# Seven quadrant products instead of eight in the second MLP product of a sparse-attention and mixer kernel

## The chip, the cores and the metric

The kernel runs on one core of a Trainium2 chip. The time is the device time of one execution in microseconds. Medians are over several executions; traces come from the hardware profiler. In a trace, PE is TensorE's matmul, PEld its weight load, DVE is VectorE, ACT ScalarE, POOL GpSimd and SP SyncE. Clock shares beside the spans are between 0.98 and 1.00 of full speed in all profiles used here but one, which is marked.

## The reference, cut to what matters

```python
# batch 4, heads 8, seq 768, head_dim 64; x = attention output, (4, 768, 512)
keep = is_global | is_local                 # 8 global keys, 96 local ones
a = softmax(where(keep, q @ k.T / 8 + bias, -1e9));  x = a @ v
h = x.transpose(0, 2, 1) @ U @ V            # U (768, 32), V (32, 768): mixer of rank 32
u = x + h.transpose(0, 2, 1)
ch = np.maximum(u @ w_ch1, 0.0) @ w_ch2     # w_ch1 (512, 2048), w_ch2 (2048, 512)
return u + ch
```

Batches are worked on one after the other. Attention of batch b+1 lies beside the MLP of batch b. Heads go in pairs, so there are 16 pairs, numbered over all batches. An evacuation is a copy of a result out of PSUM, the memory that TensorE writes to; the kernel uses PSUM as eight banks of 512 fp32 columns.

## The kernel before

Every piece of work is a `Task` with an engine, a duration, a priority and dependencies. A planner, run when the program is built, turns the tasks into one fixed instruction order per engine. Tasks that need a buffer or a PSUM bank acquire a `Group`. The framework then sets the semaphores for that order from what each instruction reads and writes. The second MLP product is one accumulation of 16 row blocks of 128 for each of six token tiles, each in a bank of its own. The residual u comes as x on VectorE and as the mixer's rank-32 part in a row-tiled matmul (one on 32 or 64 rows; several run side by side. One on 128 rows is called full-height).

```python
banks = [Group("ps", among=MLP1) for _ in units]      # a PSUM bank for each token tile
...
o = ps[:, g.slot, 0:c1 - c0]
for jc in range(lo, hi_):                             # 16 matmuls of 512 columns
    nc.tensor.matmul(o, htr[:, jc, tt * P:(tt + 1) * P], w2[:, jc, c0:c1],
                     start=False, stop=(jc == NJC - 1))
...
def rest(ahead=tuple(ahead)):                         # mixer part of the residual, 32 rows
    nc.tensor.matmul(ps[:, banks[u].slot, 0:a1 - a0], vrep[r, t2 * P:(t2 + 1) * P],
                     tb[r, a0:a1], start=True, stop=False)
...
def fin(...):                                         # one sum for each tile
    nc.vector.tensor_tensor(osb[go.slot][:, c0:c1], ps[:, g.slot, 0:c1 - c0], xb[:, tt, c0:c1], ALU.add)
```

The softmax here doesn't subtract the row's maximum and nothing guards it: scores larger than these inputs give would overflow.

## Time and profile before

| | before |
|---|---|
| median time | 242.29 us (242.01 to 242.84) |
| first matmul of the first MLP product | 33.19 us |
| start of the last matmul | 237.39 us, and 3.19 us from there to the end |
| TensorE's gaps between those two | none over 0.25 us |

A gap here, and everywhere below, is what the distance between the starts of two matmuls in a row has beyond the usual pace. It is a little more than the idle time that the views of the profile print, as matmuls overlap. What the prediction shows of this kernel is not shown again. Two more places matter later. The first is the page's throughput of DMA in 40 slices of the span (6 us each):

```profile
GB/s 172 161 181 210 114 142 199 210 174 129 159 181 196 185 161 181 117 96 38 109 155 123 142 156 157 3 0 3 2 85 48 44 87 3 0 0 4 122 53 87
```

The fifth slice, 24 to 30 us, has 114 GB/s: transfers run through the start. The second is the tail, from the timeline (start, duration, engine, line, operation, and in brackets the idle time before it):

```profile
237.34 0.96 SPq L871 DMA_DIRECT2D out_dram<-osb  x2
237.65 0.29 DVE L866 TENSOR_TENSOR osb<-ps,x_sb 128x128 f32<-128x128 f32 x1 [0.34 <-PE ps L834]
```

The last sum is of 128 columns only and its store is 64 KB.

### The profile page before, as it was taken

What the parts mean: (1) busy time and instruction counts of PE and PEld (TensorE: products, weight loads), DVE (VectorE), ACT (ScalarE), POOL (GpSimd) and SP (SyncE); (2) the same over time, 40 slices, a digit from 0 to 9 for tenths busy, and PEclk for the clock granted to TensorE, in tenths of its full rate; (3) what the DMA queues carried; (4) which work ended last, traced back from release to release, by engine and by line L of the source; (5) the groups of instructions that cost most, each with busy time, mean ns of one, the idle gap of its engine ahead of it and who ended that gap; (6) DMA issues with size and microseconds to landing.
All of it is one profiled execution on the core that took longest, in us unless ns stands there. A gap on an engine that the chain in (4) does not pass through costs nothing.

```text
span 240.6 us, 4943 instructions
## 1 busy us (share of the span) xinstructions
PE 232.8 (97%) x2092; PEld 129.8 (54%) x2092; DVE 96.7 (40%) x181; ACT 109.2 (45%) x141; POOL 91.3 (38%) x118
## 2 busy tenths in 40 slices
PE   7889799999999999999999999999999999999995
PEld 3546666566445655665545546655456456654443
DVE  5968852233364642330557852433336410001221
ACT  3786859875224028657243338567220026660000
POOL 8996994549961960190081910300001000000000
PEclk9999999999999999999999999999999999999999
DMA  8999899999999999895499996000021120000312
GB/s 172 161 181 210 114 142 199 210 174 129 159 181 196 185 161 181 117 96 38 109 155 123 142 156 157 3 0 3 2 85 48 44 87 3 0 0 4 122 53 87
DMA packets 89910, 26.39 MB, mean 110 GB/s; under 512 B 77760, under 2 KB 86912, under 8 KB 89888
## 3 DMA queue, kind: packets, MB, share of 16 engines
q0 software_dynamic: 65696, 13.24, 68.3%
q1 hardware_dynamic: 24192, 12.83, 26.2%
q8 instruction: 16, 0.26, 0.5%
q14 instruction: 6, 0.05, 0.1%
HBM read 27.46 MB, written 6.29 MB: 140 GB/s over the span
## 4 chain that ended last, share of the span: by engine, by line
PE 88%; DMA 5%; POOL 3%; DVE 2%; issue 0%; SPq 0%; POOLq 0%; DVEq 0%
PE ps L834 36%; PE ps L794 35%; PE ps L602 4%; DMA stgq<-in_q_dram 4%; PE ps L675 2%; PE ps L653 2%; PE ps L658 2%; PE ps L674 2%; PE ps L847 2%; DMA stg<-in_q_dram 2%; PE ps L754 2%; POOL x L739 1%; PE ps L895 1%; PE ps L499 1%; POOL vt L389 1%; DVE bias L340 1%
## 5 line engine op out<-in xcount | busy, mean ns | idle before, releaser
L834 PE MATMUL ps<-w,htr 128*128 128x512 f16 (+2 forms) x400 | 88.6, 371 | 0.0
L794 PE MATMUL ps<-uT,w 128*128 128x384 f16 x512 | 87.8, 326 | 0.0
L811 ACT ACTIVATE htr<-ps 128x768 f16<-128x768 f32 x64 | 51.9, 811 | 37.0 <-PE ps L794 37.0
L794 PEld LDWEIGHTS <-w 128*128 128x128 f16 x512 | 48.3, 98 | 32.0 <-issue 0.5
L613 ACT ACTIVATE ep<-ps 128x1024 f16<-128x1024 f32 (+1 forms) x48 | 44.4, 952 | 39.4 <-PE ps L602 38.0
L834 PEld LDWEIGHTS <-htr 128*128 128x128 f16 x400 | 36.1, 98 | 41.5 <-issue 3.8
L866 DVE TENSOR_TENSOR osb<-ps,x_sb 128x512 f32<-128x512 f32 (+2 forms) x25 | 16.7, 670 | 54.4 <-PE ps L834 54.2
L739 POOL CAST x<-x_sb 128x768 f16<-128x768 f32 x12 | 10.6, 888 | 53.2 <-DVE x_sb L713 25.4
L626 DVE TENSOR_TENSOR ep<-ep,mask 128x1024 f16<-128x1024 f16 x24 | 17.4, 725 | 30.6 <-ACT ep L613 30.6
L389 POOL DMA_DIRECT2D vt<-in_v_dram x16 | 16.5, 1033 | 23.7 <-PE ps L675 22.3
L296 POOL COPY vo<-vt 32x650 f16<-32x650 f16 x22 | 17.1, 782 | 6.6 <-DMA vt<-in_v_dram 6.0
L385 POOL DMA_DIRECT2D stgk<-in_k_dram x20 | 16.6, 838 | 4.1 <-DMA w<-in_moe_w_ch_dram 1.7
L385 POOL DMA_DIRECT2D stgq<-in_q_dram x20 | 16.5, 835 | 3.2 <-DMA w<-in_moe_w_ch_dram 1.7
L602 PEld LDWEIGHTS <-kT 64*128 64x128 f16 x352 | 9.9, 94 | 11.9 <-issue 10.4
L294 DVE CAST uT<-ps 128x768 f16<-128x768 f32 (+1 forms) x15 | 12.3, 845 | 8.6 <-PE ps L754 8.6
L602 PE MATMUL ps<-qT,kT 64*128 64x128 f16 x352 | 15.7, 218 | 0.0
L713 DVE TENSOR_TENSOR x_sb<-ps,rcp 128x768 f32<-128x768 f32 x16 | 15.3, 956 | 0.6
L292 ACT ACTIVATE uT<-ps 128x384 f16<-128x384 f32 (+1 forms) x5 | 2.8, 555 | 24.8 <-PE ps L754 24.8
L675 PEld LDWEIGHTS <-ep 128*128 128x128 f16 x192 | 12.4, 97 | 1.9
L675 PE MATMUL ps<-vt,ep 128*128 128x65 f16 x192 | 13.2, 193 | 0.0
L622 DVE TENSOR_TENSOR ep<-ep,mask 128x768 f16<-128x768 f16 x12 | 6.9, 573 | 14.9 <-ACT ep L613 14.9
L674 PE MATMUL ps<-vo,ep 128*128 128x65 f16 x160 | 11.9, 193 | 0.0
(57 smaller groups left out, 146.3 us busy)
## 6 DMA issues: line engine op xcount, KB each, us to landing
out_dram<-osb SPq DMA_DIRECT2D x23, 256.0 KB, 2.0
w<-in_moe_w_ch_dram POOLq DMA_DIRECT2D x8, 512.0 KB, 11.8
vt<-in_v_dram POOLq DMA_DIRECT2D x16, 192.0 KB, 8.1
stgk<-in_k_dram POOLq DMA_DIRECT2D x20, 96.0 KB, 8.7
stgq<-in_q_dram POOLq DMA_DIRECT2D x20, 96.0 KB, 7.1
vo<-vt SPq DMA_DIRECT2D x13, 121.9 KB, 6.8
stgk<-in_k_dram POOLq DMA_DIRECT2D x5, 192.0 KB, 5.1
stgq<-in_q_dram POOLq DMA_DIRECT2D x5, 192.0 KB, 5.9
```

The costliest lines, as they stand in the source:

```text
L296: nc.gpsimd.tensor_copy(dst, src)
L385: nc.gpsimd.dma_start(o[:, :, hi], src[b, h0 + hi].rearrange("(n p) d -> p n d", p=P))
L389: nc.gpsimd.dma_start(vt[gv.slot][:, :, :, 0:D], v[b, h0:h0 + 2].rearrange("h (n p) d -> p h n d", p=P),)
L602: nc.tensor.matmul(t[:, hi, j * P:(j + 1) * P], lhs, qt[r, i * P:(i + 1) * P], start=not biased, stop=True, skip_group_check=biased,)
L613: nc.scalar.activation(ep[gep.slot][:, :, lo:512], ps[:, gsc.slot:gsc.slot + 2, lo:512], AF.Exp, scale=qk_scale)
L626: nc.vector.tensor_tensor(ev, ev, mv, ALU.mult)
L674: nc.tensor.matmul(o, e[:, hi, j * P:(j + 1) * P], vof[:, hi, i - 1], start=True, stop=False)
L675: nc.tensor.matmul(o, e[:, hi, (j + 1) * P:(j + 2) * P], vv[:, hi, i], start=(i == 0), stop=True)
L794: nc.tensor.matmul(ps[:, g.slot + half, 0:HS], w1[:, dc, jt * P:(jt + 1) * P], ub[:, dc, half * HS:(half + 1) * HS], start=(dc == 0), stop ...
L811: nc.scalar.activation(htr[:, jt].rearrange("p (h c) -> p h c", h=2), ps[:, g.slot:g.slot + 2, 0:HS], AF.Relu)
L834: nc.tensor.matmul(o, htr[:, jc, tt * P:(tt + 1) * P], w2[:, jc, c0:c1], start=False, stop=(jc == NJC - 1),)
L866: nc.vector.tensor_tensor(osb[go.slot][:, c0:c1], ps[:, g.slot, 0:c1 - c0], xb[:, tt, c0:c1], ALU.add)
```

## The change

The intent is to save an eighth of the multiplications of the second product. Its three matrices are cut in halves both ways, and the 2x2 product of blocks is done with seven block products and some sums (the scheme of Strassen and Winograd). The sums of the relu's output (`sA`, and in place in `htr`), of the weights (`tB`, and in place in `w2`) and of the products are on VectorE. ScalarE takes the mixer's evacuations in the later batches, scores come in two groups a pair instead of three, the mixer's small products become full-height, and the durations of the sums in the plan are measured ones.

For each of three pairs of token tiles there are now four accumulators of 256 columns. **They lie two to a bank:** `gX` holds P1+P2 and P6, `gY` holds P7 (later P4) and P5 (later P3).

```diff
-        banks = [Group("ps", among=MLP1) for _ in units]
+        for t in range(ht):
+            gX, gY = Group("ps", 3, among=among), Group("ps", 4, among=among)
+            def half(g, i):
+                return ps[:, g.slot, i * hd:(i + 1) * hd]
 ...
+            P1 = prod(1, gX, 0, htr[:, 0:hj], w2[:, 0:hj, 0:hd], ..., 1)
+            P6 = prod(6, gX, 1, sA[:, 1], tB[:, 0], pa[0::2] + c_tb, 2)
+            P7 = prod(7, gY, 0, htr[:, 0:hj], tB[:, 1], pa[1::2] + c_ta, 3, c0=HS)
+            P5 = prod(5, gY, 1, sA[:, 0], w2[:, 0:hj, hd:DM], pa[0::2] + c_ta, 4)
+            D0 = ...  # ScalarE: u2 = P1          D1 = ...  # u2 += P6
+            D2 = ...  # u3 = P7 + u2              D4 = ...  # x22 += P5
+            P2 = prod(2, gX, 0, htr[:, hj:NJC], w2[:, hj:NJC, 0:hd], ... + [D0], 5)
+            P4 = prod(4, gY, 0, htr[:, hj:NJC], tB[:, 2], ... + [D2], 6, c0=HS)
+            P3 = prod(3, gY, 1, sA[:, 2], w2[:, hj:NJC, hd:DM], ... + [D4], 7)
+            D3 = ...  # x22 += u3                 D5 = ...  # x12, x21 += u2 (512 columns)
+            D6, D7, D8 = ...  # x11 += P1+P2, x21 += P7+P4, x12 += P5+P3
 ...
+        p1 = add(DVE, 1.16, ..., pre1, ...)   # two fp16 sums of quadrants of htr
+        p2 = add(DVE, 1.06, ..., pre2, [p1])  # two more; four times a batch
 ...
-            e = {"A": ACT, "D": DVE}[CFG.get("E", "DDD")[p]] if first else DVE
+            e = {"A": ACT, "D": DVE}[CFG.get("E", "DDD")[p] if first else CFG.get("EB", "A")]
 ...
-CFG = {'petr': (4, 5), 'cast0': 'AD', 'E': 'DAD', 'VO': 'DPPSSSSSSSSSSSSS'}
+CFG = {'petr': (4, 5, 6), 'E': 'DAD', 'VO': 'PPSSSSSSSSSSSSSS'}
```

The priorities of the plan are all new as well, so the order of nearly everything moves a little.

## The prediction

> **What bounds the kernel now.** I read the page's busy table first, then its slices, then the chain that ended last.
>
> ```profile
> PE 232.8 (97%) x2092; PEld 129.8 (54%) x2092; DVE 96.7 (40%) x181; ACT 109.2 (45%) x141; POOL 91.3 (38%) x118
> ...
> PE   7889799999999999999999999999999999999995
> ...
> PEclk9999999999999999999999999999999999999999
> ...
> PE 88%; DMA 5%; POOL 3%; DVE 2%; issue 0%; SPq 0%; POOLq 0%; DVEq 0%
> ```
>
> TensorE is at 9 tenths from the sixth slice to the last but one, at full clock, and 88% of the chain is its own work. A busy PE need not be a PE at its peak, so I looked at what it does. The groups of instructions:
>
> ```profile
> L834 PE MATMUL ps<-w,htr 128*128 128x512 f16 (+2 forms) x400 | 88.6, 371 | 0.0
> L794 PE MATMUL ps<-uT,w 128*128 128x384 f16 x512 | 87.8, 326 | 0.0
> ...
> L866 DVE TENSOR_TENSOR osb<-ps,x_sb 128x512 f32<-128x512 f32 (+2 forms) x25 | 16.7, 670 | 54.4 <-PE ps L834 54.2
> ```
>
> L834 is the second MLP product, L794 the first. Together they are 71% of the chain, with no idle time before them. The 371 ns is a latency and overlaps its neighbours, so rates must be read from start times. The waits of TensorE sum to under 5 us in the whole run, all before 33.2 us, when the first matmul of L794 starts. From there to the last matmul at 237.6 us the kernel is TensorE's queue, so a microsecond taken from TensorE there is one taken from the time, as long as the other engines keep up. The table of stretches, with the columns PE, PEld, DVE, ACT, POOL, shows their slack (first product and second product of batch 0, then of batch 1, then the second product of batch 3):
>
> ```profile
> 33.19:59.36 26.17, 26.17 (x258) 16.05 (x254) 7.58 (x14) 20.16 (x28) 16.65 (x21) 1.00 1.61 175
> 59.36:87.90 28.54, 28.54 (x235) 14.22 (x234) 14.83 (x26) 6.62 (x8) 20.31 (x25) 1.00 1.90 170
> 87.90:111.90 24.00, 24.00 (x197) 14.30 (x194) 6.00 (x11) 15.50 (x19) 8.15 (x10) 1.00 1.34 131
> 111.90:142.10 30.20, 30.20 (x291) 15.53 (x291) 18.39 (x32) 10.46 (x12) 13.61 (x16) 1.00 1.18 127
> ...
> 215.10:240.60 25.50, 22.51 (x120) 10.41 (x119) 4.31 (x7) 0.81 (x1) 0.00 (x0) 1.00 0.17 63
> ```
>
> VectorE is used for 22 of the 55 us of batch 0's MLP and 24 of the 54 us of batch 1's.
>
> The timeline of the last batch gives rates and the price of a small group:
>
> ```profile
> 230.12 3.63 PE L834 MATMUL ps<-w,htr 128*128 128x512 f16 x16
> ...
> 233.68 0.09 PEld L847 LDWEIGHTS <-vrep 32*128 32x128 f16 x2 [0.42 <-issue]
> ...
> 233.94 3.50 PEld L834 LDWEIGHTS <-htr 128*128 128x128 f16 x32 [0.17 <-issue]
> ```
>
> From 230.12 to 233.68 there are 16 matmuls and one entry into 32-row matmuls: 3.56 us. Another stretch has 56 matmuls from 217.61 to the next entry at 229.81, 12.20 us. The difference, 40 matmuls in 8.64 us, is 0.216 us for one, which leaves 0.10 us for the entry. At 217.29 two 512-column matmuls run side by side in separate row groups and the full-height ones resume at 217.61: 0.32 us less 0.216 is 0.10 us for the exit. So **each run of row-tiled matmuls costs about 0.20 us beside its columns**.
>
> **What the Trainium skill says.** "TensorE: Matmul & The Clock Gate", section "Back-to-back issue gap", has 134, 262 and 518 cycles for 128, 256 and 512 columns, 56, 109 and 216 ns at 2.4 GHz. The trace agrees where it can: 0.216 us at 512, and six 128-column matmuls with six weight loads in 0.34 us (L653); it has no 256-column one. "TensorEngine Tiling (Array Packing)", section "Key Properties", says that a change of tiling mode drains TensorE; the 0.10 us each way is that. "VectorE: DVE Perf Modes", section "The TRN2 errata — SBUF-src ops pay a fixed extra latency per instruction", gives an fp32 sum of two tensors as (N+151)/0.96 ns: 692 ns for 512, measured 691 (L866). At 256 it gives 424 ns. "SBUF — State Buffer" says that a VectorE operation with two SBUF inputs is blocked by a GpSimd operation that reads SBUF. The mask product usually takes 0.69 us, but 1.16 at 69.56 us, beside a GpSimd copy: agrees.
>
> **The change part by part.** All on TensorE after 33 us.
>
> 1. Second product, per batch: 6 token tiles x 16 matmuls x 0.216 = 20.7 us becomes 7 products x 3 tiles x 8 = 168 matmuls of 256 columns, at 0.109 (estimate, between 0.0555 for 128 and 0.1625 for 384 columns of L794) = 18.3 us. Four batches: 83.0 - 73.2, **-9.8 us**. The eighth saved would be 10.4; the rest is the fixed cost of twice-as-many, smaller matmuls.
> 2. Residual products (L847): 13 groups of parallel 32-row matmuls at 0.216 = 2.8 us become 12 groups of four full-height 256-column ones at 0.436 = 5.2: **+2.4**.
> 3. Mixer product (L754): 12 after 33 us, from two 384-column matmuls side by side (0.163) to two in sequence (0.326): **+2.0**.
> 4. Pair 6 gets its transposes on TensorE in place of DMA: 24 of about 0.033 (such a set takes 0.79 at 32.4 us): **+0.8**.
> 5. Row-tiled runs: after 33.2 us I count 39 on TensorE's timeline: 25 with scores, 14 of residual or mixer products alone. The latter become full-height and stop being runs. Scores of batches 1 to 3 come in two groups a pair instead of three: 24 at most, some adjacent, say 22. 17 x 0.20: **-3.4**.
>
> Sum: -9.8 + 2.4 + 2.0 + 0.8 - 3.4 = **-8.0 us**. Note that 2 and 3 are paid for by 5, so nearly all of the eighth survives.
>
> VectorE pays. Per batch: 16 sums of two fp16 quadrants of 768 elements (0.55 us, like the 0.57 of the 768-element mask product) = 8.9; per tile seven 256-element fp32 sums at 0.42 and one of 512 at 0.65 = 3.6, for three tiles 10.8; off go six 0.69 sums (4.2) and three mixer evacuations of 0.95 in batches 1 to 3 (2.9), which ScalarE takes at 0.81. Batch 1: 24.4 + 8.9 + 10.8 - 7.1 + 0.3 = 37 of now about 52 us. Batch 0 adds the sums of the second weights (8 of 0.7: 5.6): 41 of about 53, 78%. In all VectorE goes from 97 to about 155 us, ScalarE from 109 to about 121. Neither becomes the bound on average.
>
> At the ends: the tail has a 0.42 us sum in place of 0.29 and a store of 128 KB in place of 64: **+0.3**. In the first 33 us, where VectorE is busy for 25, the four 0.82 us vrep casts (3.3) give way to four half-length pieces (about 1.9) and an early memset: **-0.3**, uncertain in sign.
>
> **The rivals.**
>
> A: *VectorE becomes the bound locally.* For: batch 0's second product needs both weight-sum sets, which wait for the last of the w loads, and has the densest attention work beside it; about 27 us of VectorE work falls in 26 us there if little is moved ahead; GpSimd copies and casts collide with the new two-SBUF-input sums, as at 69.56 us. VectorE is a strict queue: one sum waiting for a product holds the masks behind it. Against: only 7.6 us of VectorE in the 26 us before, PSUM groups allow the first products of two tiles (plain operands) to run first, and the order was planned with these durations. I charge **+1.0 us** in the centre; if it went badly, 4 to 6 us, a time of 238 to 240.
>
> B: *256-column matmuls don't reach 0.109*, because each now needs its own 98 ns weight load. Were the pace 0.12, 672 x 0.011 = 7.4 us of gain is gone: about 241. Against: L653 sustains one load and one matmul in 0.056 us. Unlikely.
>
> C: *The start decides*: any lateness of the first L794 comes through in full. The plan's priorities are all different, so +-1 us.
>
> D: *First products of a batch wait for the last relu and its sums.* About 0.3 + 0.81 + 1.16 and hand-overs, some 2.7 us, against residual, first and second plain products of two tiles, 4.3 us, on TensorE. Hidden, even in batch 3 where no attention fills in.
>
> **The number.** 242.3 - 8.0 + 0.3 - 0.3 + 1.0 = 235.3, which I round to 235.2 (2.9% faster). Spread: +-0.8 us for the runs of row mode, +-1 for the start, -1 to +4 for VectorE waits: 232.6 to 238.6 should hold it 8 times in 10. Faster by over 2% means under 237.4; only rival A or B at size prevents that: 0.80. Within 2%: 0.18. Slower: 0.02.
>
> **What would show it.** 672 matmuls of 256 columns with starts 0.108 to 0.11 us apart (step 1); no 32-row matmuls and 20 to 24 row-tiled runs after the start (2, 3, 5); VectorE at 145 to 165 us busy; TensorE still without gaps from 33 us on, waits on VectorE under 2 us in total (A), the first L794 within 1 us of 33.2 (C). I am wrong if TensorE waits on VectorE for more than 3 us, if the fp16 sums take well over 0.6 us, or if the first product starts much later.

## The result, and the profile after

The median is 240.49 us (239.86 to 240.64) against 242.15 us of the kernel before in the same rounds. The ratio is 0.9923, with a 95% interval of 0.9893 to 0.9952. Ratios here are the mean time of one kernel's fast runs over that of the other's fast runs of the same rounds, so not quite the ratio of the medians quoted. The change is 0.8% faster, within 2%, and the time lies above the predicted range.

The page of the kernel after, busy times first, then the DMA throughput and the engines of the chain that ended last:

```profile
PE 226.9 (95%) x2436; PEld 165.8 (69%) x2436; DVE 146.8 (62%) x317; ACT 122.9 (52%) x165; POOL 90.6 (38%) x116
...
GB/s 169 167 131 137 39 166 200 201 209 187 164 154 168 206 184 191 175 103 61 119 58 164 128 164 195 0 3 0 3 1 91 88 90 2 0 3 0 0 91 176
...
PE 70%; DMA 17%; DVE 8%; issue 1%; POOL 1%; SPq 0%; DVEq 0%; ACT 0%; POOLq 0%
```

TensorE's share of the chain fell from 88% to 70%, while DMA rose from 5 to 17 and VectorE from 2 to 8. TensorE's own part of the time did shrink, and waits took most of it back. What TensorE waited for in the whole run (total, times, longest), the largest lines:

```profile
PE ps L734 <- DMA vo<-vt: 2.2, 1, 2.2
PE ps L934 <- DVE x_sb L947: 1.5, 2, 1.0
...
PE ps L934 <- DVE w L508: 0.9, 1, 0.9
...
PE ps L855 <- DVE x_sb L947: 0.3, 1, 0.3
PE ps L934 <- DVE u L947: 0.3, 1, 0.3
```

L934 is the second product, L855 the first, L947 the sums of products, L508 a sum of weights. The first line lies before the MLP starts. The others are waits of TensorE on VectorE, 3.0 us, inside the part that had none before. Counted from start to start there are six gaps, 4.16 us: 1.04 at 65.1 us (the weight sum), and 0.46, 0.54, 0.29, 1.15 and 0.68 at 123.3, 141.2, 188.0, 190.3 and 227.5 us (sums of products; for the one at 188.0 us this view names no releaser).

From the start times, with the measured sizes beside the predicted ones:

| step | predicted, us | measured, us |
|---|---|---|
| second product, without waits (mean pace of each size times its count: 83.2 and 73.4) | -9.8 | -9.8 |
| all else of TensorE after the start (residual, mixer, pair 6, runs of row-tiled matmuls) | +1.8 | +1.5 |
| waits on VectorE | +1.0 | +4.16 |
| first matmul of the first MLP product | -0.3 | +1.07 (34.26 against 33.19) |
| from the last matmul's start to the end | +0.3 | +1.06 (4.25 against 3.19) |
| sum | -7.0 | -2.0 (the spans are 238.6 and 240.6) |

The table of stretches, for the second product of batches 0 and 1 (columns as in the prediction):

```profile
59.10:89.10 30.00, 29.13 (x373) 24.31 (x371) 28.45 (x60) 11.67 (x16) 25.65 (x31) 1.00 2.02 177
112.60:141.80 29.20, 28.59 (x366) 24.33 (x365) 22.82 (x51) 11.85 (x17) 13.28 (x15) 1.00 1.20 120
```

VectorE is busy for 28.45 of 30.00 us in the second product of batch 0 (and for 10.49 of the 24.84 us before it, so 71% of the two; the prediction counted 78%). Yet none of the five gaps on sums of products is in batch 0. They lie in batches 1 to 3, where VectorE has room. The timeline of the last one, in batch 3 where no attention is left, shows why:

```profile
225.02 1.04 PE L934 MATMUL ps<-w,sA 128*128 128x256 f16 x8
...
225.90 1.04 PE L934 MATMUL ps<-w,htr 128*128 128x256 f16 x8
226.10 0.42 DVE L947 TENSOR_TENSOR u<-ps,u 128x256 f32<-128x256 f32 x1 [0.38 <-PE ps L934]
...
226.77 1.04 PE L934 MATMUL ps<-tB,htr 128*128 128x256 f16 x8
...
227.84 0.76 DVE L947 TENSOR_TENSOR x_sb<-ps,x_sb 128x256 f32<-128x256 f32 x2 [0.72 <-PE ps L934]
228.32 0.93 PE L934 MATMUL ps<-w,sA 128*128 128x256 f16 x7 [0.52 <-DVE x_sb L947]
```

The product at 225.02 is P5, in the second half of `gY`. It ends at 226.06, and the sum at 226.10 starts just then; but this sum (D2) reads P7 in the first half, which had ended at 224.3, and VectorE had been idle for 0.38 us. P4 follows at 226.77, into the first half. The sum that reads P5 (D4) could have run once VectorE was free, but it starts at 227.84, just after P4's end at 227.81, with VectorE idle for 0.72 us. P3, which must follow D4, so starts late. A sum of one half waits for the product that writes the other half, and the next product into the bank waits for the sum. The wait at 190.3 us is of the same kind: P4 of that tile, which needs only D2 (ended at 190.71), starts at 191.56, just after the sum of the other half ended at 191.51:

```profile
187.27 0.69 DVE L970 TENSOR_TENSOR x_sb<-x_sb,u 128x512 f32<-128x512 f32 x1
187.88 0.42 DVE L947 TENSOR_TENSOR x_sb<-ps,x_sb 128x256 f32<-128x256 f32 x1
...
188.35 1.03 PE L934 MATMUL ps<-tB,htr 128*128 128x256 f16 x8
...
190.29 0.42 DVE L947 TENSOR_TENSOR u<-ps,u 128x256 f32<-128x256 f32 x1 [1.74 <-PE ps L934]
...
191.09 0.42 DVE L947 TENSOR_TENSOR x_sb<-ps,x_sb 128x256 f32<-128x256 f32 x1
...
191.56 1.03 PE L934 MATMUL ps<-tB,htr 128*128 128x256 f16 x8 [0.98 <-DVE x_sb L947]
```

The five gaps are not all alike. Before those at 141.2, 190.3 and 227.5 us VectorE stood idle for 1.17, 1.74 and 0.72 us, though the product that its next sum reads had ended 0.9 us or more before that sum began. The one at 141.2 us is indirect: the late sum (D7) holds up the sum behind it in VectorE's queue, and that one frees the bank for the next batch. Before the gaps at 123.3 and 188.0 us VectorE had no pause of over 0.1 us in the 1.6 us before the wait ended. There the shared bank is why TensorE must wait for that sum at all (P3 for D2, and P7, at 188.35, for D4), and the work ahead of the sum in VectorE's queue is why it comes late.

"PSUM — Partial Sum Buffer" of the Trainium skill has the likely reason in its section "PSUM bank collisions raise a hardware error": two engines must not be in one bank and quadrant at the same time, even in disjoint columns, and the rule is "Semaphore-guard PSUM by **bank × quadrant** (by bank is the simple version), not by address". The waits in the trace are what one would expect of guards set by bank. This is the theory called BANK in the records below. Its rival LOAD says that VectorE is too full, and that sums come late because others stand before them.

The tail, from the same timeline of the kernel after:

```profile
232.47 3.43 SPq L978 DMA_DIRECT2D out_dram<-x_sb  x5
...
233.56 1.04 PE L934 MATMUL ps<-w,sA 128*128 128x256 f16 x8
234.63 0.76 DVE L947 TENSOR_TENSOR x_sb<-ps,x_sb 128x256 f32<-128x256 f32 x2 [1.32 <-PE ps L934]
```

Two sums, not one, wait for the last matmul; one of them reads the other half of the bank, whose product had ended 0.9 us earlier. Five stores are issued in the last microseconds, and a sum of 256 columns with 256 KB behind it takes the place of one of 128 with 64 KB.

The start, from the chain in order of time (start, duration, what):

```profile
16.76 4.11 DMA vo<-vt
...
26.74 0.97 DVE x_sb L773
27.75 0.09 issue
27.84 0.82 POOL x L799
28.65 0.70 POOL w L443
29.35 7.88 DMA w<-in_moe_w_ch_dram
```

The first weights are issued by GpSimd at 28.6 us, behind a cast that hangs on attention's results. The last line shown is the second of these loads; from there the chain runs over later loads to the weight sum before the gap at 65 us. The page has 39 GB/s in the fifth slice, against 114 before. The kernel before issues its first weights at 12.2 us, and they land at 21.35; here they land at 34.03. The theory START says that the order of the loads costs the microsecond.

### The profile page after: what moved, and what is told of

It reads as the page before. It is cut to its first block, busy times and chain, and to the rows that moved or that the text cites. A ratio compares the mean times of both kernels' runs of the same rounds, so it can differ in the third digit from the quotient of the medians.

```text
span 238.6 us, 5808 instructions
## 1 busy us (share of the span) xinstructions
PE 226.9 (95%) x2436; PEld 165.8 (69%) x2436; DVE 146.8 (62%) x317; ACT 122.9 (52%) x165; POOL 90.6 (38%) x116
## 4 chain that ended last, share of the span: by engine, by line
PE 70%; DMA 17%; DVE 8%; issue 1%; POOL 1%; SPq 0%; DVEq 0%; ACT 0%; POOLq 0%
PE ps L934 29%; PE ps L855 27%; DMA w<-in_moe_w_ch_dram 11%; PE ps L646 3%; DMA vt<-in_v_dram 3%; PE ps L735 2%; PE ps L922 2%; DMA vo<-vt 2%; PE ps L734 2%; DMA sA<-in_q_dram 2%; PE ps L813 2%; PE ps L718 2%; PE ps L713 2%; DVE x_sb L947 1%; DVE x_sb L773 1%
## 5 line engine op out<-in xcount | busy, mean ns | idle before, releaser
L855 PE MATMUL ps<-uT,w 128*128 128x384 f16 x512 | 86.4, 326 | 0.3 <-DVE x_sb L947 0.3
L855 PEld LDWEIGHTS <-w 128*128 128x128 f16 x512 | 48.8, 98 | 32.3 <-issue 0.3
L934 PEld LDWEIGHTS <-htr 128*128 128x128 f16 x384 | 36.7, 98 | 6.9 <-issue 1.5
L934 PEld LDWEIGHTS <-sA 128*128 128x128 f16 x288 | 27.7, 98 | 6.0 <-issue 2.0
L947 DVE TENSOR_TENSOR x_sb<-ps,x_sb 128x256 f32<-128x256 f32 x48 | 19.4, 420 | 12.8 <-PE ps L934 12.1
L889 DVE TENSOR_TENSOR sA<-htr 128x768 f16<-128x768 f16 x16 | 8.9, 556 | 29.4 <-ACT htr L872 29.3
L934 PE MATMUL ps<-w,sA 128*128 128x256 f16 x192 | 24.6, 272 | 1.7 <-DVE w L508 0.9
L934 PE MATMUL ps<-tB,htr 128*128 128x256 f16 x192 | 24.7, 273 | 1.1 <-DVE x_sb L947 1.0
L934 PE MATMUL ps<-w,htr 128*128 128x256 f16 x192 | 24.8, 273 | 0.0
L304 ACT ACTIVATE uT<-ps 128x768 f16<-128x768 f32 (+1 forms) x14 | 10.1, 719 | 26.1 <-PE ps L813 26.1
L397 POOL DMA_DIRECT2D stgq<-in_q_dram x18 | 14.8, 833 | 4.3 <-DMA w<-in_moe_w_ch_dram 4.3
L397 POOL DMA_DIRECT2D stgk<-in_k_dram x18 | 14.9, 834 | 2.8 <-DMA w<-in_moe_w_ch_dram 2.8
```

Of the source, the lines that this page charges most:

```text
L397: nc.gpsimd.dma_start(o[:, :, hi], src[b, h0 + hi].rearrange("(n p) d -> p n d", p=P))
L855: nc.tensor.matmul(ps[:, g.slot + half, 0:HS], w1[:, dc, jt * P:(jt + 1) * P], ub[:, dc, half * HS:(half + 1) * HS], start=(dc == 0), stop ...
L934: nc.tensor.matmul(o, a[:, j, c0 + cols.start:c0 + cols.stop], bq[:, j], start=False, stop=(j == hj - 1), skip_group_check=True,)
L947: return lambda: e.tensor_tensor(o(), x(), y(), ALU.add)
```

## The experiments

Fifteen runs were made, three of them repeats. Runs of one set ran on the same chip beside the kernel before, whose medians were 242.54, 242.50, 242.61 and 242.43 us in the four sets. Profiles are of state fast unless marked.

### First set: what TensorE waits for

**own_banks**: for the last batch, where no attention needs banks, each accumulator gets a bank of its own. The sums and the result stay. The order was meant to stay too, but the planner, run again with the new banks, moved the last three products of one pair of token tiles, with their sums and stores, ahead of all products of another pair. Within each pair of tiles the order is unchanged.

```diff
-            gX, gY = Group("ps", 3, among=among), Group("ps", 4, among=among)
+            if b == B - 1:   # one bank for each accumulator
+                gs = [Group("ps", r, among=among) for r in (2, 1, 2, 2)]
+            else:
+                gX, gY = Group("ps", 3, among=among), Group("ps", 4, among=among)
+                gs = [gX, gX, gY, gY]
```

> The changed kernel, same order of all instructions, right result; in the last batch alone each of the four accumulators of a token tile gets its own PSUM bank, where two shared one (eight banks are free there). Theory BANK: a sum that reads one half of a bank waits for the product that is writing the other half, and the next product into the bank waits for that sum. Then TensorE's 0.5 us idle gap at 228.3 us goes, the second-row sum of the last tile no longer waits for the last product (one sum instead of two after the last matmul), and the time falls by 0.7 to 1.4 us against the changed kernel (240.5 to about 239.4, ratio to before about 0.988). Theory LOAD (VectorE simply has too much in its queue): nothing in VectorE's work changes, so the gap and the time stay (240.3 to 240.7).

Measured: 238.66 us, ratio 0.9859 (0.9832 to 0.9886), right result. The gap of 0.68 us in the last batch is gone; the four in batches 1 and 2 stand as before (0.47, 0.54, 0.29, 1.14). The timeline of the last batch:

```profile
227.74 1.04 PE L940 MATMUL ps<-w,htr 128*128 128x256 f16 x8
...
228.54 0.75 DVE L953 TENSOR_TENSOR x_sb<-ps,x_sb 128x256 f32<-128x256 f32 x2
228.62 1.04 PE L940 MATMUL ps<-tB,htr 128*128 128x256 f16 x8
...
232.11 1.04 PE L940 MATMUL ps<-w,sA 128*128 128x256 f16 x8
232.31 0.43 DVE L953 TENSOR_TENSOR x_sb<-ps,x_sb 128x256 f32<-128x256 f32 x1 [0.45 <-PE ps L940]
```

Sums now run beside products, and TensorE starts its products without a gap. At the end only one sum is left behind the last matmul, and from that matmul's start to the end it is 3.59 us instead of 4.25. The two together are 1.34 us, 0.55%. The kernel after stands at 0.9923 and 0.9895 in its two measurements, 0.991 on average, so 0.9854 was to be expected; 0.9859 was measured. The gap at 65 us is absent here too, though nothing was changed there, so the two totals do not compare only the last batch. What carries the argument is the timeline: in the pair of tiles that had the gap, and in the last one, products and sums come in the same order as before, and the sums no longer wait for the product of the other half. For the last batch BANK is shown by that; a part of the moved products in the gain isn't excluded.

**no_presum** (wrong result on purpose): the 16 fp16 sums ahead of the products of each batch are left out, and the products read `htr` instead.

```diff
             def pre1(...):
+                return
             def pre2(...):
+                return
```

> Wrong result on purpose. The changed kernel, same order, but the fp16 sums of hidden-activation quadrants are left out (64 instructions, 37 us of VectorE) and the products read the plain activations. LOAD: with a quarter of VectorE's work gone TensorE's waits on VectorE (about 4 us by start-to-start times) nearly all go, and the time falls by 3 us or more, to 237.5 or less. BANK: the sums behind the products, which share banks, still wait as before; less than 1.5 us falls away, mostly in batch 0, to 239 or more.

Measured: 239.48 us, 0.9883 (0.9859 to 0.9907). VectorE's busy time fell from 146.8 to 114.4 us. TensorE's waits on sums of products in this kernel:

```profile
PE ps L936 <- DVE x_sb L949: 1.5, 2, 1.0
...
PE ps L855 <- DVE x_sb L949: 0.3, 1, 0.3
PE ps L936 <- DVE u L949: 0.3, 1, 0.3
```

They are those of the kernel after to the tenth, and the five gaps agree to 10 ns (0.46, 0.54, 0.29, 1.15, 0.68). Taking away a fifth of VectorE's work moved none of them, so they do not come from its total load. The sums left out end about 7 us or more before each gap (at 116.4, 169.4 and 217.3 us in batches 1 to 3 of the kernel after), so the run says nothing of the few instructions just ahead of a gap. Only the gap of 1.04 us on the weight sum went.

**no_wsum** (wrong on purpose): the eight sums of weights are left out.

```diff
     def build_t(g, part):
         def go():
+            return
```

> Wrong result on purpose. The changed kernel, same order, but the eight sums of second-weight quadrants (5.5 us of VectorE) are left out and the products read the plain weights. Theory WEIGHTS: the 1.0 us gap at 66.3 us, and VectorE's jam before it, come from the last part of the weights landing at 60.6 us (52.2 before the change) and the sums on it; the time falls by 1 to 2 us, to 238.5 to 239.5. If instead BANK or the order of VectorE's queue makes that gap, it stays, and the time changes by less than 0.5 us.

Measured: 239.81 us, 0.9895 (0.9874 to 0.9915), the five gaps as ever, and a time just above the range that WEIGHTS gave. The gap at 65 us is gone, but later runs show that this says little: it is also absent from own_banks and from the second profile of the kernel after.

**thin_sums** (wrong on purpose): the sums of products are done on 8 columns only.

```diff
-                return lambda: e.tensor_tensor(o(), x(), y(), ALU.add)
+                return lambda: e.tensor_tensor(o()[:, 0:8], x()[:, 0:8], y()[:, 0:8], ALU.add)
```

> Wrong result on purpose. The changed kernel, same order and waits, but the sums behind the products handle 8 columns instead of 256 (about 43 us of VectorE becomes about 15). LOAD: TensorE's waits on VectorE nearly go, the time falls by 3 us or more (237.5 or less). BANK: the sums still start only when the product into the other half of the bank ends, and TensorE's wait shrinks only by the sum's shorter duration, 0.25 us for each of some 5 gaps: the time falls by 1 to 2 us, to 238.5 to 239.5, and two sums still follow the last matmul.

Measured: 237.75 us, 0.9808 (0.9785 to 0.9832). The gaps are down to 1.57 us (0.78 at the weight sum, 0.37, 0.42). The time lies between the ranges of BANK (238.5 to 239.5) and LOAD (237.5 or less), so it decides nothing: a wait that a bank causes has the sum itself in it and shrinks with it. The timeline says more. Before the last gap VectorE is idle for 1.50 us and its short sum still starts only at the end of the other half's product, and two sums still start after the last product's end (232.71 and 232.79 us), as BANK has it. The gaps at 123.3, 141.2 and 188.0 us go, among them the two that have VectorE's queue in them.

### Second set: the tail, the start, and a plan that knows the banks

**own_tail**: own_banks, and the store of the last row block cut in two, so that its first half goes ahead of the last sum.

```diff
+            if b == B - 1 and t == ht - 1:
+                add(SP, 0.35, 0, store(t + ht, hd, DM), [D3], ...)
+                osb_done[b].append(add(SP, 0.35, 0, store(t + ht, 0, hd), [D7], ...))
```

> Right result. The run with own banks in the last batch, and the last tile's second-row store split in two, so that its right half leaves before the last sums. Theory TAIL: after the changed kernel's last matmul, 0.5 MB of stores leave within 2.6 us, and the last 256 KB store is what ends late; with 128 KB left at the end the stretch from the last matmul's start to the end shrinks from 3.6 us (own banks) to 3.1 to 3.3, the time by 0.2 to 0.5 us against own banks (238.66 to about 238.3). If the end is the fixed time of a store after the last sum, no change within 0.2 us.

Measured: 238.87 us, 0.9844 (0.9794 to 0.9894). From the last matmul's start to the end it is 3.50 us against 3.59 of own_banks, so the 3.1 to 3.3 of TAIL were missed. The intervals overlap widely, so a gain of the split in the time isn't shown.

**w1_early**: the kernel after with the loads of three quarters of the first weights ahead of the values of pair 4.

```diff
     order = pl.run()
+    w1s = [t for t in order if t.name in ("w1_0", "w1_1", "w1_2")]
+    order = [t for t in order if t not in w1s]
+    at = [t.name for t in order].index("lv4")
+    order[at:at] = w1s
```

> Right result. The changed kernel with one edit of GpSimd's queue: the first three loads of the first weights are issued ahead of the values of pair 4 (at about 26 us instead of 28.6). Theory START: the first weights land at 34.0 us and hold the first product, and the later loads behind them hold the second weights' sums; the first product then starts 0.3 to 0.6 us earlier (33.7 to 33.9), the second weights' last part lands before 59 us, the 1.0 us gap at 66 us goes, and the time falls by 0.8 to 1.8 us. If the start hangs on the attention chain before it (its last mixer evacuation ended at 33.9), the first product stays at 34.2 or later and only the gap may go: 0 to 1 us.

Measured: 240.56 us, 0.9914 (0.9883 to 0.9945), so nothing gained. The weights landed at 30.66 us, and yet the first matmul of the MLP came at 34.96 us: the chain of attention ahead of it ended at 34.57 us. The landing of the weights and attention's chain end close together, and bringing one forward shows the other.

**bp_best1** and **bp_best2**: own_tail with a planner that keeps sums and products of a bank apart, and with priorities searched anew; two results of that search.

```diff
+        wrote, read = [0.0] * 8, [0.0] * 8           # for each bank: end of the last product, sum
 ...
+                        if t.bank is not None and e == PE:
+                            r = max(r, read[t.bank.slot] + 0.2)
+                        elif t.bank is not None:
+                            r = max(r, wrote[t.bank.slot] + 0.3)
 ...
+            if t.bank is not None:
+                (wrote if t.eng == PE else read)[t.bank.slot] = t.end
```

> Right result. The kernel of own_tail, with the bank rule put into the plan that orders the instructions: a product waits for the sums that read its bank and a sum for the products that write it, whichever half; and the priorities searched anew with that rule. BANK: the four gaps of batches 1 and 2 (2.4 us in the changed kernel, 0.46, 0.54, 0.29, 1.15) nearly go, TensorE's gaps after its first product come to under 1 us, and the time is 236 to 237.5, 2 to 2.6% under before. LOAD: other gaps take their place, and the time stays at 238 to 239. This plan starts the first product late and puts attention of later batches before it, so its weak point is the DMA loads.

> Right result. As bp_best1 with other priorities from the same search, first product near its old place. BANK: gaps under 1 us, 236 to 237.5. LOAD: 238 to 239. If the two differ by over 1.5 us, the place of the loads in the first 45 us is worth that much beside the banks.

Measured, bp_best1: 236.05 us (235.22 to 237.09), 0.972 (0.9677 to 0.9764), right result, faster than both kernels. TensorE's gaps are 0.80 us in sum, none of them on a sum of products. Its busy times and its chain, from the page:

```profile
PE 225.6 (97%) x2419; PEld 164.9 (71%) x2419; DVE 149.8 (64%) x317; ACT 122.9 (53%) x165; POOL 90.0 (39%) x116
...
PE 83%; DMA 9%; POOL 5%; issue 1%; DVE 1%; ACT 0%; SPq 0%
```

VectorE does 3 us more than in the kernel after, and its share of the chain is down from 8% to 1%. The work is the same but for the own banks of the last batch and one store; it lies in another order.

bp_best2 measured 241.44 us, 0.9931 (0.99 to 0.9963), outside both ranges given, with a profile in the slow state (clock 0.979). It has no gap on sums of products either. Its first MLP matmul is at 39.31 us, with 2.87 us of waits for weights behind it. So a plan may be good in the middle and lose it all at the start; its loads come too late.

### Third set: repeats, one part undone, and a control

**after_again**: the kernel after, unchanged.

> The changed kernel, unaltered, for its time beside the others of this job and a second look at its gaps. All theories: ratio to before 0.990 to 0.996; the gaps of batches 1 to 3 (0.46, 0.54, 0.29, 1.15, 0.68 us) the same to some 10 ns; the first product between 33.8 and 35.1 us, as in the runs that kept its order.

Measured: 240.03 us, 0.9895 (0.9843 to 0.9946), just outside the range expected, as is the first product. The same five gaps (0.46, 0.54, 0.29, 1.14, 0.68), so they belong to the order. There is no gap at 65 us, and the first MLP matmul is at 35.54 us instead of 34.26. Still both profiles begin the MLP of batch 1 at 89.1 us and both spans are 238.6 us: where the start is early, the last weights and their sums are what is late. The two losses stand in for one another in these two profiles.

**e_on_dve**: the evacuations of the mixer in batches 1 to 3 go back to VectorE.

```diff
-                copy(e, uT[b % 2][:, hp]..., ps[:, gx.slot:gx.slot + 2, 0:HS])
+                copy(DVE if not first else e, uT[b % 2][:, hp]..., ps[:, gx.slot:gx.slot + 2, 0:HS])
```

> Right result. The changed kernel, same order, with the nine mixer evacuations of batches 1 to 3 back on VectorE (0.95 us each) instead of ScalarE (0.81). LOAD: VectorE gets 8.6 us more and TensorE's waits on it grow by 2 us or more, time 242 or more. BANK: VectorE's load matters little, the gaps change by less than 1 us in sum and the time by less than 1 us (240 to 241.3).

Measured: 241.40 us, 0.9953 (0.9936 to 0.997), and gaps of 5.02 us. Against after_again on the same chip it is 0.6% slower, about 1.4 us by the medians, though the intervals just overlap. The gap at 188.0 us grew from 0.29 to 1.02 us: an evacuation of 0.94 us now stands ahead of the sum that it waits for. The one at 190.3 us, with VectorE idle before it, stayed at 1.15. So VectorE's queue has its price where the sums stand close. Of the expectations it meets neither in full: more than BANK alone, less than LOAD.

**start_both**: w1_early, and the values of pair 2 shifted by VectorE copies, not by the DMA that TensorE waits for at 18 to 21 us.

```diff
+            if p == 2:
+                for c in range(0, PO, 32):
+                    copy(DVE, vo[gv.slot][c:c + 32], vt[gv.slot][c + 32:c + 64, :, 0:NB - 1])
+                return
```

> Right result. The changed kernel, same order, with the first weights' loads issued before the values of pair 4 (as in w1_early) and the shifted values of pair 2 copied by VectorE instead of by a DMA that TensorE waits for at 18 us until 18.6 to 20.9. Theory START: both hold the first product, each alone is hidden by the other (w1_early moved the landing to 30.7 and the first product stayed at 35.0 behind an attention chain that ended at 34.6); together they bring it to 32.6 to 33.6, and the time falls by 0.8 to 1.8 us (239 to 240). If neither is the cause, it stays above 34.

Measured: 241.18 us, 0.9948 (0.993 to 0.9966). The first MLP matmul is at 35.96 us, not earlier, so the expectation failed. The first weights landed at 32.01 us, but attention's last evacuation ended only at 35.56, against 32.8 to 34.4 in the runs with the start of after. The run doesn't show what early weights alone would bring.

**ctl_search**: own_tail with priorities searched just as long, but without the bank rule; a control for bp_best1.

> Right result. Control for the new priorities: the kernel of own_tail with priorities searched as long and in the same way as for bp_best1, but without the bank rule in the plan. BANK: gaps of TensorE in batches 0 to 2 stay at 2 us or more in sum and the time at 238 to 239.5. If the search alone brought bp_best1's gain, gaps fall under 1 us and the time to 236 to 237.

Measured: 237.69 us, 0.9779 (0.9745 to 0.9814), gaps of 0.33 us, **and a wrong result that was not intended** (relative error 0.031). Its cause was looked for in the plan and not found. The expectation of at least 2 us of gaps failed: an order found without the rule avoids the bank waits too. What took the waits away is another order; that the rule in the planner is needed is not shown. A run with a wrong result is a weak control, and this stays open.

### Fourth set: is the loss at the start real

**before_again**: the kernel before, unchanged, one look.

> The kernel before, unchanged, for a second profile. The first profile of it has its first row product of the first MLP layer at 33.19 us; the theory that the change costs about 1 us at the start needs this to be near 33.2 again (within 0.4 us). If it lies between 34 and 35.5 us, as in the runs with the order of after, then the start differs from run to run and no loss at the start can be put down to the change. Sum of gaps on TensorE's row under 1 us after its first first-layer product, in either case.

Measured: 242.2 us, one run, state unknown. The first MLP matmul is at 33.03 us, no gap. The two profiles of before have 33.0 and 33.2 us. The eight with the loads and the start of the kernel after (after, after_again, own_banks, own_tail, no_presum, no_wsum, thin_sums, e_on_dve) have 33.8 to 35.5 us, 34.7 on average. So the new order does start later, by some 1.6 us on average, and it varies more. The landings of the first weights, read from the traces, say what sets it. In seven of the eight the first MLP matmul starts 0.04 to 0.05 us after that landing (33.78 to 35.49 us); in after they land at 34.03 and the last scores before the MLP end at 34.26. Without the weights it could have followed those scores, at 34.0 us on average (an estimate: the start of the last score matmul plus 0.15 us, as in after). That puts about 0.9 us of the 1.6 on attention's chain and 0.7 on the landing.

**best_w1**: bp_best1 with the first quarter of the first weights loaded ahead of two transposed input blocks and a load of values.

```diff
+    order.insert([t.name for t in order].index("XC2"), w10)
+    order.insert([t.name for t in order].index("XC1") + 1, lv4)
```

> The best plan so far with the first quarter of the first weights loaded ahead of two transposed input blocks and a value load. If the landing of the first weights alone sets its start, the first first-layer product comes at 32.6 to 33.0 us instead of 33.5 and the time falls by 0.5 to 0.9 us against the best plan of the same rounds. If the chain of attention in front of it sets the start too, as two runs that moved loads in after's order suggested, the first product stays at 33.4 to 34.5 us and the time does not move (within 0.3 us).

**bp_best1_again**: bp_best1, unchanged.

> The best plan once more, beside the other two: 0.972 of the kernel before, between 0.968 and 0.977, the first first-layer product at 33.3 to 33.9 us, and gaps of TensorE under 1 us in sum, if its gain is a property of the order; a ratio above 0.98 would say that the earlier figure was a lucky chip.

Measured, best_w1: 237.17 us, 0.98 (0.9767 to 0.9834). Its first MLP matmul is at 33.36 us, but 1.18 us are lost at 35.8 us to the next quarter of the weights and 1.59 us at 57.3 us to attention's VectorE work. The load ahead didn't help. bp_best1_again: 236.38 us, 0.975 (0.9714 to 0.9787), right, gaps of 0.65 us, first MLP matmul at 34.5 us (expected 33.3 to 33.9, so that part was missed). The gain of bp_best1 holds on a second chip; its early start does not.

## Why the prediction was wrong

- **Step 1 was right**: -9.8 us, as said. The 256-column matmuls start 0.109 us apart, so rival B is refuted. (Its "about 241" doesn't add up: 7.4 us on 235.2 are 242.6.)
- **Steps 2 to 5 were right in sum**: +1.5 us against +1.8. The row-tiled runs after the start went from 39 to 22, as counted, and no 32-row matmul is left. TensorE's part, without waits, shrank by 8.3 us, and -8.0 was predicted. The single steps 2 to 5 were not measured apart.
- **VectorE's sizes were right**: 146.8 us busy, 145 to 165 said; fp16 sums of 0.55 to 0.62 us (means of their four lines), fp32 sums of 256 columns 0.42.
- **The step that failed is rival A**, charged with +1.0 us; it measured 4.16 us in the first profile and 3.11 in the second. The prediction's own test ("if TensorE waits on VectorE for more than 3 us") says so. Its cause was wrong as well. It looked for a VectorE too full, in batch 0. Of the six gaps only the 1.04 us at the weight sum is of that sort, and it comes and goes. At the other five, 3.1 us, two accumulators share a bank; at two of them (0.75 us) the length of VectorE's queue has its part too. The prediction set against A that "PSUM groups allow the first products of two tiles (plain operands) to run first"; it didn't ask what shares a bank. It could have: the diff has `half(g, 0)` and `half(g, 1)` of one slot, and the rule on guards by bank, quoted above, was there to be read. For the last batch the cause is shown (own_banks, with its moved products). For the four gaps of batches 1 and 2 it is argued from their timelines, and e_on_dve shows the queue's part at one; no run gave those their own banks.
- **The start was mis-sized**: -0.3 us said, with the sign called uncertain; +1.07 in the first pair of profiles, about +1.6 on average. The instruments of rival C were right (its limit of 1 us was passed), and what the MLP waited for is known: the landing of the first weights, in seven of eight profiles. But loads moved early (w1_early, start_both, best_w1) bring the landing forward and not the time, because attention's chain ends close behind. Why that chain ends later than in the kernel before is not known.
- **The tail was mis-sized**: +0.3 us said, +1.06 measured. The sum was counted as one of 0.42 us in place of 0.29 and the store as twice the size; the bank puts a second sum behind the last matmul and more stores come at the end. Own banks took 0.66 us of it back.
- **D was right**: no gap at the start of a second product.

Rival A by 3.2 us, the start by 1.4 and the tail by 0.8 are over by 5.3 us together. TensorE's part gave back 0.3 us. That makes the 5.0 us between -7.0 and -2.0.

Open are why attention's chain ends later at the start, the wrong result of ctl_search, and whether bp_best1 owes its gain to the rule or to a lucky order.

## What to carry to other kernels

When a product is cut into more, smaller accumulators, count who else lives in each PSUM bank: in these kernels a reader of one half waited for the writer of the other half, and the writer for the reader, even with both engines free. A wait on an engine is not yet a wait for its load. See whether that engine is idle just before the instruction waited for; if it is, look for what the two share, and if not, at what stands ahead of it. Where a plan is made from durations and dependencies alone, put that sharing into the plan or search for an order again: here nearly the same instructions in another order, with own banks in the last batch, took the ratio from 0.991 to 0.972 and 0.975.

## What the Trainium skill lacked or had wrong

- "PSUM — Partial Sum Buffer", section "PSUM bank collisions raise a hardware error", gives guarding by bank as the simple version and says nothing of its price in time. Here the gaps at shared banks were of 0.29 to 1.15 us, 3.1 us in a run of 238.6; banks of their own in the last batch took away 0.68 us of these and 0.66 us at the end.
- "TensorEngine Tiling (Array Packing)", section "Key Properties", says that a change of tiling mode drains TensorE and gives no time. The trace of the kernel before has about 0.10 us each way.
